# Turning x of the second half of the rows on VectorE and through a DRAM scratch instead of on TensorE

## The chip, the cores and the metric

The kernel runs on one core of a Trainium2 chip. The metric is the device time of one execution in microseconds (us). Before the change it is 1184.43 us, the median of 3 runs (1184.28 to 1184.72). The profile was taken from another execution of the same program, of 1184.46 us; the span from its first to its last instruction is 1182.7 us.

A core has five engines with an instruction queue each, and each queue is worked off in order: TensorE (PE in the profile, its weight loads PEld), VectorE (DVE), ScalarE (ACT), GpSimd (POOL) and SyncE (SP), which here does nothing but issue transfers (DMAs). Matmul results land in PSUM, which only VectorE and ScalarE empty in this kernel.

## The reference

One transformer layer with an attention branch and a feed-forward branch in parallel, 2048 rows of width 576, all in float32:

```python
xn  = layernorm(x)                       # over the 576 columns, no weights
qkv = xn @ wqkv                          # 576 x 1728; 32 heads of width 18
# every row attends to 8 keys: itself and the rows 2, 4, ..., 14 before it
logits = einsum(q, k at those rows) * 18 ** -0.5     # -1e9 before row 0
o   = softmax(logits) @ (v at those rows)
out = x + o @ wo + relu(xn @ w1) @ w2    # w1: 576 x 4608, w2: 4608 x 576
```

The attention looks back in steps of 2, so rows of even and of odd number never meet.

## The kernel before, in words

**Two parities.** The rows are worked in two halves (`ph` 0 and 1, the two parities of the row number), one after the other. A half has 8 tiles of 128 rows (`i`), taken in pairs as 4 token blocks of 256 rows (`tb`).

**Three products for one.** Every float32 operand is split into a high part (rounded to the type `fp32r`, on ScalarE) and a low part (what is left, by a subtraction on VectorE). A product is high x high + low x high + high x low. The width 576 is 4 blocks of 128 and 64 columns over; the last 64 are held twice in one block, as high and low (`mix`). One product over 576 is so 14 matmuls, in the order of the list `TERMS`: high parts of the moving side first, low parts after them, and so on.

**Slots.** The work is written out by hand as 288 slots, `slots[n]`: for each half, 12 chunks (`c`) of the 36 blocks of the 4608 hidden columns, for each chunk 4 token blocks, for each of these 3 hidden blocks (`f`). Half 1 begins with slot 144. In step n TensorE does the hidden product of slot n + 2 (`h_mm`, 14 matmuls into `ph`, PSUM, 2 buffers) and the output product of slot n (`o_mm`, 12 matmuls into `po`, PSUM). Between them ScalarE takes `hhi` (relu, L476) and VectorE `hlo` (L477) out of `ph`; the hidden product of slot m + 2 needs the buffer that these two release in slot m. After every third slot VectorE adds two `po` banks to x in place (L500), which releases them to the next slot's output product.

**What lies beside.** Into the slots are put, by the tables `at` (ahead of the output product) and `late` (after it): the q, k, v products; the attention itself, on VectorE (`run_bg`, as much as an estimate of VectorE's and TensorE's times allows); the product with `wo`; the loading and splitting of weights, staged three ahead in a pool of four buffers (`st`); and the making of the next half's x.

**The product with wo (slots 123 to 136 of half 0).** The attention's output for tile i has to be turned. `wo_a` turns it in 32 x 32 blocks on VectorE into the tile `tr` (L417, L418; one buffer), and four DMAs write `tr` to a DRAM scratch (`turned`) so that the blocks end up in their places (L424). `wo_f`, a slot later, reads the scratch back (L431). `wo_s`, at the end of the slot after that, splits what came into high (ScalarE, L438) and low (VectorE, L439, L440). `wo_b`, in the next slot, is the product: 28 matmuls into two `pm` banks, of which the first 8 read the high part and the next 8 the low part, and VectorE adds both to x (L453). `wo_a` of tiles 6 and 7 stands in slots 132 and 133, `wo_s` of them in 134 and 135, `wo_b` in 135 and 136. A new `wo_a` may write `tr` only when the four writes of the one before have landed.

**x of half 1 (slots 126 to 150).** For tile i, with z = 135 + 2i: the load in slot z - 6; the row statistics (`stats`) at the end of slot z - 2: four VectorE instructions (L245 twice, L246, L247), and on GpSimd the negated mean (L249) and the power -1/2 of the variance (L250); the normalising on VectorE (`norm`, L261) a slot later, so that GpSimd's part has a slot's time; and in slot z + 1 `make_xt`: five transposes on TensorE (L275, L276) into `pm`, a copy for the high part on ScalarE (L278, L280) and a subtraction on VectorE for the low (L279, L281). They go into `XT`, of which four are held, one for each token block; half 1 takes a block's buffer over as soon as half 0's last hidden product from it is done. Half 1's first hidden products, from token block 0, stand in step 142, those of block 1 in step 145, then 148 and 151.

Of the kernel before, what the change touches and what calls it, by code (L numbers as in the profile page):

```python
# [10 lines left out]
F32 = mybir.dt.float32  # L11
F32R = mybir.dt.float32r
AF = mybir.ActivationFunctionType
ALU = mybir.AluOpType
# [3 lines left out]
P = 128  # L18
# [3 lines left out]
TBN = 256  # L22
W = 8
# [4 lines left out]
EPS = 1e-5  # L28

UNIT0, UNIT_STEP, WO_AT = 7, 27, 8  # L30
WO_STEPS = (0, 1, 3, 4, 6, 7, 9, 10)
HEADW = (-5, -2, -1, 0, 0, 1)

# [23 lines left out]
def tile_body(ctx: ExitStack, tc: tile.TileContext, x, wqkv, wo, w1, w2, out):  # L57
    nc = tc.nc
    S, D = x.shape
    F = w1.shape[1]  # L60
    Dh = 18
    UD = HG * Dh
    NF = F // P
    NCH = NF // C
    KT = 4
    DR = D - KT * P
# [27 lines left out]
    f32 = lambda ap: ap.bitcast(F32)  # L94
# [22 lines left out]
    def dve(n):  # L117
        t["dve"] += (n + 130) / 960.0
# [112 lines left out]
    X, XT, XN, MR = {}, {}, {}, {}  # L231
# [34 lines left out]
    def transpose_split(src, last, hi, mix, lo, free=False):  # L266

        if free:
            pa, pb = (ps_o.tile([P, 2, 512], F32, name="po")[:, 0, :] for _ in range(2))
            pa, pb = pa.rearrange("p (k c) -> p k c", k=KT), pb[:, 0:P]  # L270
        else:
            pa = ps_m.tile([P, KT, P], F32, name="pm")
            pb = ps_m.tile([P, P], F32, name="pm")
        for k in range(KT):
            nc.tensor.transpose(pa[:, k, :], src[:, k * P : (k + 1) * P], ident)  # L275
        nc.tensor.transpose(pb, last, ident)  # L276
        t["pe"] += 5 * 0.06
        nc.scalar.activation(hi, pa, AF.Copy)  # L278
        nc.vector.tensor_tensor(lo, pa, f32(hi), op=ALU.subtract)  # L279
        nc.scalar.activation(mix, pb, AF.Copy)  # L280
        nc.vector.tensor_tensor(mix[DR:P], pb[DR:P], f32(mix[DR:P]), op=ALU.subtract)  # L281
        dve(512)
        dve(128)

    def make_xt(ph, i, free=False):
        tb, h = divmod(i, 2)
        if h == 0:
            XT[ph, tb] = xtp.tile([P, 9, TBN], F32R, name="xT")
        d = XT[ph, tb][:, :, h * P : (h + 1) * P]
        xn = XN.pop((ph, i))  # L290
        transpose_split(xn[:, 0:512], xn[:, 512:640], d[:, 0:4, :], d[:, 4, :], d[:, 5:9, :], free)


    TERMS = [(k, k) for k in range(KT)] + [(5 + k, k) for k in range(KT)] + [(4, 4)] + [(k, 5 + k) for k in range(5)]


    QO, KK, VV = {}, {}, {}

    def qkv_tile(ph, u, i):
# [106 lines left out]

    OT = {}

    TD = {}

    def wo_a(ph, i):


        assert (ph, i) in ready, (ph, i, len(bg))
        o = QO[ph][:, i, :]
        tr = tmp.tile([P, 640], F32, name="tr", bufs=1)
        nc.vector.transpose(tr[:, 0:D], o)  # L417
        nc.vector.transpose(tr[:, D:640], o[:, KT * P : D])  # L418
        dve(D)
        dve(DR)  # L420
        TD[ph, i] = turned.tile([5 * 4, 32, P], F32, name="turned")
        for r in range(4):
            rows = slice(32 * r, 32 * r + 32)
            nc.sync.dma_start(  # L424
                TD[ph, i][:, :, rows].rearrange("g j i -> j g i"),
                tr[rows, :].rearrange("j (g i) -> j g i", i=32),
            )

    def wo_f(ph, i):
        OT[ph, i] = tmp.tile([P, 5, P], F32R, name="xn", bufs=3)  # L430
        nc.sync.dma_start(f32(OT[ph, i]), TD.pop((ph, i)).rearrange("(k c) j i -> (c j) k i", k=5))  # L431

    def wo_s(ph, i):

        r = OT[ph, i]
        z = f32(r)
        d = tmp.tile([P, 5, P], F32R, name="oT", bufs=1)
        nc.scalar.activation(d, z, AF.Copy)  # L438
        nc.vector.tensor_tensor(r[:, 0:KT], z[:, 0:KT], f32(d[:, 0:KT]), op=ALU.subtract)  # L439
# [3 lines left out]
        OT[ph, i] = [d[:, k] for k in range(5)] + [r[:, k] for k in range(4)]  # L443
# [64 lines left out]
    def at(n, f, *a):  # L508
        todo.setdefault(n, []).append((f, a))
# [3 lines left out]
    def late(n, f, *a):  # L513
        todo_late.setdefault(n, []).append((f, a))

    plan = []
    for ph in range(NPH):
        b = ph * SPP
        for c in range(NCH):
            for f in range(C):  # L520
                s = b + c * SPC + f
                first = ph == c == 0
                plan.append((HEADW[f] if first else s - 5, w1_task, ((ph, c, f), c * C + f)))
                plan.append((HEADW[3 + f] if first else s - 3, w2_task, ((ph, c, f), c * C + f)))
        for u in range(NU):
            s = b + UNIT0 + u * UNIT_STEP
            plan.append((s - 5, wq_tasks, ((ph, u), u)))
            for i in range(NI):
                at(s + i, qkv_tile, ph, u, i)
            late(s + NI + 1, attention, ph, u)  # L530
        s = b + UNIT0 + NU * UNIT_STEP + WO_AT
        plan.append((s - 8, wo_tasks, (ph,)))
        for i in range(NI):
            z = s + WO_STEPS[i]
            late(z, wo_a, ph, i)
            at(z + 1, wo_f, ph, i)
            late(z + 2, wo_s, ph, i)
            at(z + 3, wo_b, ph, i)
            at(z + 3, done, ph, i)
        if ph + 1 < NPH:  # L540
            e = b + SPP - SPC
            for i in range(NI):
                z = e + 3 + 2 * i
                at(z - 6, load_x, ph + 1, i)
                late(z - 2, stats, ph + 1, i)
                late(z - 1, norm, ph + 1, i)
                at(z + 1, make_xt, ph + 1, i)
    for step, f, a in sorted(plan, key=lambda z: z[0]):
        if f in (wq_tasks, wo_tasks):
            f([step + k for k in range(5)], *a)  # L550
# [67 lines left out]
```

## Time and profile before

| what | value |
|---|---|
| median of 3 runs | 1184.43 us (1184.28 to 1184.72) |
| the profiled execution | 1184.46 us, span 1182.7 us |
| TensorE busy | 1174.6 us, 99% of the span, 8936 matmuls |
| VectorE busy | 822.3 us, 70%, 1301 instructions |
| ScalarE busy | 306.9 us, 26%, 758 instructions |
| GpSimd busy | 40.1 us, 3%, 63 instructions |
| the 56 + 14 transposes into `pm`, the 8 + 2 into `po` (both halves) | first at 6.5 us, the last at 623.9 us |
| writes to the scratch (L424) | 64, 80 KB each, 2.3 us from issue to landing (median) |
| reads from it (L431) | 16, 320 KB each, 3.2 us |

The profile's lines name an engine, a line of the kernel (L275), the operation, and what is written from what (`pm<-ident,xn`); behind them stand busy time and mean duration, or, in a timeline, the start and the length of a stretch of like instructions, in us from the span's start. In square brackets stands how long the engine was idle just before and who ended that. "PEclk" is the clock that TensorE was granted, as a share of the full one. Busy times of TensorE are modelled from pipelined matmuls, so lengths of neighbouring stretches overlap a little, and it is the distance of their starts that counts.

### The profile page before, as it was taken

What the parts mean: (1) busy time and instruction counts of PE and PEld (TensorE: products, weight loads), DVE (VectorE), ACT (ScalarE), POOL (GpSimd) and SP (SyncE); (2) the same over time, 40 slices, a digit from 0 to 9 for tenths busy, and PEclk for the clock granted to TensorE, in tenths of its full rate; (3) what the DMA queues carried; (4) which work ended last, traced back from release to release, by engine and by line L of the source; (5) the groups of instructions that cost most, each with busy time, mean ns of one, the idle gap of its engine ahead of it and who ended that gap; (6) DMA issues with size and microseconds to landing.
All of it is one profiled execution on the core that took longest, in us unless ns stands there. A gap on an engine that the chain in (4) does not pass through costs nothing.

```text
span 1182.7 us, 21731 instructions
## 1 busy us (share of the span) xinstructions
PE 1174.6 (99%) x8936; PEld 1164.9 (98%) x8936; DVE 822.3 (70%) x1301; ACT 306.9 (26%) x758; POOL 40.1 (3%) x63
## 2 busy tenths in 40 slices
PE   8999999999999999999999999999999999999998
PEld 8999999999999999999999999999999999999998
DVE  7516885888687668877673288758777884787852
ACT  5422222131222211322233123121322222222210
POOL 2000000010000000000020000000100000000000
PEclk9999999999999999999999999999999999999999
DMA  5312121130312211356342122121302213114541
GB/s 174 85 32 79 39 84 47 47 108 1 99 45 58 65 55 44 104 112 148 105 131 74 47 55 80 32 77 27 98 21 80 70 43 89 47 30 110 115 100 60
DMA packets 137364, 86.16 MB, mean 73 GB/s; under 512 B 48832, under 2 KB 120768, under 8 KB 137264
## 3 DMA queue, kind: packets, MB, share of 16 engines
q1 hardware_dynamic: 134736, 76.58, 24.0%
q10 hardware_dynamic: 2528, 8.20, 2.4%
q8 instruction: 70, 1.15, 0.4%
q14 instruction: 30, 0.25, 0.1%
HBM read 66.58 MB, written 9.96 MB: 65 GB/s over the span
## 4 chain that ended last, share of the span: by engine, by line
PE 95%; DVE 2%; DMA 2%; ACT 0%; SPq 0%; issue 0%; POOL 0%; DVEq 0%; ACTq 0%
PE ph L114 37%; PE po L114 37%; PE pm L114 20%; DMA st<-in_w 1%; DMA xn<-turned 1%; PE pm L275 0%; DVE pr L382 0%; DMA turned<-tr 0%; DVE x L500 0%; DMA x<-in_x 0%; DVE pr L345 0%; SPq L424 0%; DVE w1t L145 0%; DVE w2t L145 0%; DVE bst L245 0%
## 5 line engine op out<-in xcount | busy, mean ns | idle before, releaser
L114 PE MATMUL ph<-xT,w1t 128*128 128x256 f32 x4032 | 513.0, 278 | 1.3 <-ACT xT L278 0.6
L114 PEld LDWEIGHTS ph<-xT,w1t 128*128 128x128 f32 x4032 | 491.9, 188 | 2.1 <-ACT xT L278 0.8
L114 PE MATMUL po<-w2t,hhi 128*128 128x288 f32 x2304 | 400.7, 296 | 0.6 <-DVE w2t L145 0.3
L114 PEld LDWEIGHTS po<-w2t,hhi 128*128 128x128 f32 x2304 | 336.9, 188 | 2.4 <-issue 0.5
L476 ACT ACTIVATE hhi<-ph 128x256 fp32r<-128x256 f32 x288 | 110.1, 382 | 553.5 <-PE ph L114 538.2
L114 PE MATMUL po<-w2t,hlo 128*128 128x288 f32 x1152 | 244.7, 293 | 0.0
L477 DVE SCALAR_TENSOR_TENSOR hlo<-ph,hhi 128x256 fp32r<-128x256 f32 x288 | 121.5, 422 | 161.0 <-ACT hhi L476 160.1
L500 DVE TENSOR_TENSOR x<-po,x 128x576 f32<-128x576 f32 x192 | 143.4, 756 | 69.9 <-PE po L114 67.0
L114 PE MATMUL pm<-wq,xT 128*128 128x432 f32 x896 | 185.5, 358 | 0.0
L114 PEld LDWEIGHTS po<-w2t,hlo 128*128 128x128 f32 x1152 | 183.6, 188 | 0.0
L114 PEld LDWEIGHTS pm<-wq,xT 128*128 128x128 f32 x896 | 163.8, 188 | 5.6
L145 DVE TENSOR_TENSOR w2t<-st,w2t 128x576 fp32r<-128x576 f32 x72 | 54.3, 755 | 45.6 <-ACT w2t L148 45.4
L345 DVE TENSOR_TENSOR pr<-qo,k 128x1152 f32<-128x1152 f32 x64 | 85.8, 1349 | 0.0
L348 DVE TENSOR_REDUCE lg<-pr 128x64 f32<-128x1152 f32 x64 | 84.9, 1343 | 0.0
L375 DVE TENSOR_TENSOR pr<-lg,v 128x1152 f32<-128x1152 f32 x64 | 84.7, 1350 | 0.2
L382 DVE TENSOR_TENSOR pr<-pr 128x288 f32<-128x288 f32 (+1 forms) x128 | 70.6, 601 | 0.1
L145 DVE TENSOR_TENSOR w1t<-st,w1t 128x640 fp32r<-128x640 f32 x72 | 59.0, 820 | 13.8 <-ACT w1t L148 13.7
L148 ACT ACTIVATE w2t<-st 128x576 fp32r<-128x576 f32 x72 | 49.1, 683 | 57.2 <-PE po L114 42.4
L314 ACT ACTIVATE k<-pm 128x144 f32<-128x144 f32 x64 | 18.6, 291 | 143.9 <-PE pm L114 143.9
L148 ACT ACTIVATE w1t<-st 128x640 fp32r<-128x640 f32 x72 | 53.0, 736 | 11.4 <-DMA st<-in_w 11.4
L351 POOL TENSOR_SCALAR_AFFINE_SELECT lg<-lg 1x512 f32<-1x512 f32 x8 | 9.4, 1171 | 844.1 <-DVE lg L348 844.1
L114 PE MATMUL pm<-wq,oT 128*128 128x288 f32 x224 | 35.2, 296 | 0.3 <-ACT oT L438 0.3
(61 smaller groups left out, 444.7 us busy)
## 6 DMA issues: line engine op xcount, KB each, us to landing
st<-in_w SPq DMA_DIRECT2D x72, 288.0 KB, 3.0
st<-in_w SPq DMA_DIRECT2D x72, 256.0 KB, 3.0
st<-in_wqkv SPq DMA_DIRECT2D x32, 216.0 KB, 3.0
turned<-tr SPq DMA_DIRECT2D x64, 80.0 KB, 2.3
xn<-turned SPq DMA_DIRECT2D x16, 320.0 KB, 3.2
st<-in_w SPq DMA_DIRECT2D x144, 32.0 KB, 2.7
out<-x SPq DMA_DIRECT2D x16, 288.0 KB, 2.1
x<-in_x SPq DMA_DIRECT2D x15, 288.0 KB, 3.6
```

Of the source, the lines that this page charges most:

```text
L114: nc.tensor.matmul(o, l, r, start=start, stop=stop)
L145: nc.vector.tensor_tensor(lo, src, f32(hi), op=ALU.subtract)
L148: nc.scalar.activation(hi, src, AF.Copy)
L314: nc.scalar.activation(k[:, W - 1 + i, :], pq[:, 1, :], AF.Copy)
L345: nc.vector.tensor_tensor(pr[i], q, window(k, i), op=ALU.mult)
L348: nc.vector.tensor_reduce(lg[:, i], pr.pop(i).rearrange(heads, d=Dh), axis=AX.X, op=ALU.add)
L351: nc.gpsimd.affine_select(out=z, in_=z, pattern=[[1, NI], [1, W], [0, HG]], compare_op=ALU.is_ge, fill=-1e9 / scale, base=1 - W, channel_m ...
L375: nc.vector.tensor_tensor(pr[i].rearrange(heads, d=Dh), e, window(v, i).rearrange(heads, d=Dh), op=ALU.mult)
L382: nc.vector.tensor_tensor(o, z[:, 0:n], z[:, n : 2 * n], op=ALU.add)
L476: nc.scalar.activation(hi, pt, AF.Relu)
L477: nc.vector.scalar_tensor_tensor(lo, pt, 0.0, f32(hi), op0=ALU.max, op1=ALU.subtract)
L500: nc.vector.tensor_tensor(acc, PO[k][:, :, 0:D2], acc, op=ALU.add)
```

## The change

For half 1 the five TensorE transposes of every tile are replaced by the way that `wo` already goes: `turn` (two VectorE transposes into `tr`, four DMAs to the scratch) and `fetch` (one DMA back, straight into `XT`). `xt_s` then splits what lies in `XT` in place. The table `XT_STEPS` says, for every tile, how far from slot 132 (`e`) the load, the statistics with the normalising, the turning (`send`), the reading back (`back`) and the splitting (`parts`) stand. Statistics and normalising, a slot apart before, stand one behind the other in the same slot. The normalised x lies in a buffer of the attention's products (`pr`) instead of `xn`. The pool of x tiles has 12 buffers instead of 11, the scratch 4 instead of 3. In `XT` and in `wo`'s split tile high and low parts change places, and `TERMS` with them, so that every product still has the same 14 matmuls on the same parts in the same order. Half 0's x is still turned on TensorE.

```diff
+XT_STEPS = (
+    (-6, 0, 0, 2, 6),
+    (-5, 1, 2, 4, 8),
+    (-3, 2, 3, 5, 9),
+    (-1, 4, 5, 7, 11),
+    (4, 6, 7, 9, 13),
+    (5, 8, 9, 11, 14),
+    (7, 10, 11, 13, 16),
+    (8, 11, 12, 14, 17),
+)
...
-    xp = pool("xp", 11)
+    xp = pool("xp", 12)
...
-    turned = pool("turned", 3, space=bass.MemoryType.DRAM)
+    turned = pool("turned", 4, space=bass.MemoryType.DRAM)
...
+    def turn(o, td):
+        tr = tmp.tile([P, 640], F32, name="tr", bufs=1)
+        nc.vector.transpose(tr[:, 0:D], o)
+        nc.vector.transpose(tr[:, D:640], o[:, KT * P : D])
+        dve(D)
+        dve(DR)
+        for r in range(4):
+            rows = slice(32 * r, 32 * r + 32)
+            nc.sync.dma_start(
+                td[:, :, rows].rearrange("g j i -> j g i"),
+                tr[rows, :].rearrange("j (g i) -> j g i", i=32),
+            )
+
+    def fetch(z, td):
+        nc.sync.dma_start(z, td.rearrange("(k c) j i -> (c j) k i", k=5))
+
+    def norm_turned(ph, i):
+        nm, r = MR.pop((ph, i))
+        XN[ph, i] = prp.tile([P, W, UD], F32, name="pr").rearrange("p w c -> p (w c)")[:, 0:D]
+        nc.vector.tensor_scalar(XN[ph, i], X[ph, i], nm, r, op0=ALU.add, op1=ALU.mult)
+        dve(600)
+
+    def xt_a(ph, i):
+        TD[ph, i] = turned.tile([5 * 4, 32, P], F32, name="turned")
+        turn(XN.pop((ph, i)), TD[ph, i])
+
+    def xt_f(ph, i):
+        tb, h = divmod(i, 2)
+        if h == 0:
+            XT[ph, tb] = xtp.tile([P, 9, TBN], F32R, name="xT")
+        fetch(f32(XT[ph, tb][:, 0:5, h * P : (h + 1) * P]), TD.pop((ph, i)))
+
+    def xt_s(ph, i):
+        tb, h = divmod(i, 2)
+        d = XT[ph, tb][:, :, h * P : (h + 1) * P]
+        z = tmp.tile([P, 5, P], F32R, name="oT", bufs=1)[:, 0]
+        mix = d[:, 4, :]
+        nc.scalar.activation(d[:, 5:9, :], f32(d[:, 0:4, :]), AF.Copy)
+        nc.vector.tensor_tensor(d[:, 0:4, :], f32(d[:, 0:4, :]), f32(d[:, 5:9, :]), op=ALU.subtract)
+        nc.scalar.activation(z[DR:P], f32(mix[DR:P]), AF.Copy)
+        nc.vector.tensor_tensor(mix[DR:P], f32(mix[DR:P]), f32(z[DR:P]), op=ALU.subtract)
+        nc.scalar.activation(mix[0:DR], f32(mix[0:DR]), AF.Copy)
+        dve(512)
+        dve(128)
...
             e = b + SPP - SPC
             for i in range(NI):
-                z = e + 3 + 2 * i
-                at(z - 6, load_x, ph + 1, i)
-                late(z - 2, stats, ph + 1, i)
-                late(z - 1, norm, ph + 1, i)
-                at(z + 1, make_xt, ph + 1, i)
+                load, first, send, back, parts = (e + k for k in XT_STEPS[i])
+                at(load, load_x, ph + 1, i)
+                late(first, stats, ph + 1, i)
+                late(first, norm_turned, ph + 1, i)
+                late(send, xt_a, ph + 1, i)
+                at(back, xt_f, ph + 1, i)
+                at(parts, xt_s, ph + 1, i)
```

More of the change, by code (lines that the diff above doesn't have):

```diff
@@ L290, in make_xt @@
         xn = XN.pop((ph, i))
[L291 to L294 removed]
+        transpose_split(xn[:, 0:512], xn[:, 512:640], d[:, 5:9, :], d[:, 4, :], d[:, 0:4, :], free)
+    TERMS = (
+        [(5 + k, k) for k in range(KT)] + [(k, k) for k in range(KT)] + [(4, 4)]
+        + [(5 + k, 5 + k) for k in range(KT)] + [(4, 9)]
+    )
[10 more added lines that the diff above has]
+                tr[rows, :].rearrange("j (g i) -> j g i", i=32),
+            )
+    def fetch(z, td):
[25 more added lines that the diff above has]
+        dve(128)
+    TD = {}
     QO, KK, VV = {}, {}, {}
@@ L407, in tile_body @@
     OT = {}
-    TD = {}
     def wo_a(ph, i):
         assert (ph, i) in ready, (ph, i, len(bg))
[L415 to L420, printed above, removed]
-        TD[ph, i] = turned.tile([5 * 4, 32, P], F32, name="turned")
[L422 to L427, printed above, removed]
+        TD[ph, i] = turned.tile([5 * 4, 32, P], F32, name="turned")
+        turn(QO[ph][:, i, :], TD[ph, i])
     def wo_f(ph, i):
         OT[ph, i] = tmp.tile([P, 5, P], F32R, name="xn", bufs=3)
-        nc.sync.dma_start(f32(OT[ph, i]), TD.pop((ph, i)).rearrange("(k c) j i -> (c j) k i", k=5))
+        fetch(f32(OT[ph, i]), TD.pop((ph, i)))
     def wo_s(ph, i):
@@ L442, in wo_s @@
         dve(128)
-        OT[ph, i] = [d[:, k] for k in range(5)] + [r[:, k] for k in range(4)]
+        OT[ph, i] = [r[:, k] for k in range(KT)] + [d[:, KT]] + [d[:, k] for k in range(KT)]
     def wo_b(ph, i):
```

## The prediction

> **What bounds the kernel now.** I read the busy times first, then who kept TensorE waiting, then the timeline of the stretch that the change touches (slots 131 to 151, about 541 to 627 us).
>
> ```profile
> PE 1174.6 (99%) x8936; PEld 1164.9 (98%) x8936; DVE 822.3 (70%) x1301; ACT 306.9 (26%) x758; POOL 40.1 (3%) x63
> ...
> PE pm L275 <- DVE x L453: 0.4, 1, 0.4
> ```
>
> TensorE is the bound: the waits that its list names come to 2.4 us once it has begun, and 0.4 us of that lies in the stretch in question (second line). So a matmul taken away is time won, and any wait that TensorE gets in its place is time lost. TensorE's timeline, start and length in us:
>
> ```profile
> 580.13 1.78 PE L114 MATMUL ph<-xT,w1t 128*128 128x256 f32 x14
> 581.75 0.60 PE L275 MATMUL pm<-ident,xn 128*128 128x128 f32 x4
> 582.19 0.27 PE L276 MATMUL pm<-ident,xn 128*128 128x128 f32 x1
> 582.22 0.78 PE L114 MATMUL po<-w2t,hhi 128*128 128x288 f32 x4
> ...
> 583.89 1.78 PE L114 MATMUL ph<-xT,w1t 128*128 128x256 f32 x14
> ...
> 587.09 1.78 PE L114 MATMUL ph<-xT,w1t 128*128 128x256 f32 x14
> ```
>
> From one hidden product to the next a slot with transposes takes 3.75 us (583.89 - 580.13), one without 3.20 (587.09 - 583.89). Then VectorE and TensorE around the last products with wo, and VectorE's load in six slots further on (busy, instructions, clock, DMA):
>
> ```profile
> 504.58 0.20 DVE L418 STREAM_TRANSPOSE tr<-qo 128x64 f32<-128x64 f32 x1
> ...
> 508.51 0.78 DVE L417 STREAM_TRANSPOSE tr<-qo 128x576 f32<-128x576 f32 x1 [1.68 <-DMA turned<-tr]
> ...
> 553.01 0.20 DVE L418 STREAM_TRANSPOSE tr<-qo 128x64 f32<-128x64 f32 x1
> ...
> 562.80 0.68 DVE L439 TENSOR_TENSOR xn<-xn,oT 128x512 fp32r<-128x512 f32 x1
> ```
>
> ```profile
> 563.54 1.22 PE L114 MATMUL pm<-wq,oT 128*128 128x288 f32 x8
> 564.60 1.23 PE L114 MATMUL pm<-wq,xn 128*128 128x288 f32 x8
> ```
>
> ```profile
> 583.89:603.00 19.11, 15.25 (x32) 1.00 0.48 151
> ```
>
> The first two lines show a turning held up, since `tr` has one buffer: from the end of L418 (504.78) until the writes have landed and L417 may start again, 3.73 us. The third is wo tile 6's turning, done at 553.21. The low part of tile 6 is ready at 563.48 (L439) and wanted at 564.60: only 1.1 us to spare. And in the six slots from 583.89 VectorE is already busy for 15.25 of 19.11 us.
>
> **What goes.** The transposes of eight tiles: seven slots shrink by 0.55 us, and the first (slot 136, 568.85 to 576.95, 8.10 us, against 6.91 for the one ahead of it, 561.93 to 568.85) by 1.19, the 0.4 us wait included: 7 x 0.55 + 1.19 = **5.0 us won**, all on TensorE.
>
> **What is added at no price.** ScalarE's three instructions for a tile (0.60, 0.27, 0.26 us) become three of such sizes, and it is 26% busy. SP issues five more DMAs for each tile (4 x 0.51 + 0.38 = 2.4 us, 20 us in some 50); behind them stand weight loads, staged three ahead and landing in 3.0 us, and outputs. I take 0; without that cover, one landing too late costs at most 1 us, and nothing of it can win time. The read back stands 3 to 5 slots (9.6 us and more) ahead of the split and lands in 3.2 us; the splits stand two slots and more ahead of the first use; `XT`'s buffers are free two slots before. The `pr` buffers are free: the last attention instruction ahead of slot 132's work ends at 547.99.
>
> **First wait: tile 6 of wo, slots 132 to 135.** VectorE's order in slot 132 becomes: wo tile 6's turning, x tile 0's statistics and normalising, x tile 0's turning; in slot 133 wo tile 7's turning, x tile 1's statistics and normalising; and only at the end of slot 134 tile 6's L439. Three turnings now follow on one `tr`. The trip from the end of a turning to the free `tr` is 3.73 us (504.78 to 508.51; by the read that waits for the same writes, 553.21 to 556.94 and 1142.46 to 1146.20) to 4.26 (558.86 to 563.12); mean of five, 3.93. From 553.21: trip 3.93; turning 0.90 (552.31 to 553.21); trip 3.93 (hlo and two L453 hide in it), so wo tile 7 turns at 561.97. Then 0.90; statistics 1.21 (558.78 to 559.99); a wait for GpSimd of 0.7, because the normalising now follows at once (L250's 0.57 and two hand-overs); normalising 0.55; hlo 0.37; two L500 1.34; L439 0.68: 567.7. Wanted at 564.60, so TensorE waits **3.1 us** (2.7 by the short trips, 3.8 by the long). The read of tile 6, now behind eight writes on SP's queue, lands at about 563.2 and its high part is ready near 564.0, 0.5 after TensorE wants it; that wait lies inside the 3.1.
>
> **Second wait: the bank release in slot 143.** From hlo in slot 138 on VectorE has work without a break. Up to slot 143's first L500, which releases the bank that slot 144's output product writes: 6 hlo at 0.35, 4 splits at 1.05 (576.08 to 577.13), 3 statistics with GpSimd's wait and the normalising at 2.50, 3 w1 subtractions at 0.75, 3 of w2 at 0.68, 2 turnings at 0.82, two L500 1.34 and one 0.75: 2.1 + 4.2 + 7.5 + 2.25 + 2.04 + 1.64 + 2.09 = 21.8 us. The hlo starts 2.2 us after its slot (576.95 to 579.16), and slot 144's output product 6 x 3.20 + 1.61 = 20.8 us after it, so there are 18.6 us: TensorE waits **3.2 us** (2.5 to 3.6, for 0.1 us more or less in each of the splits and hand-overs). Before, the six slots held three tiles' work, without the waits for GpSimd. The backlog goes on: slot 146's L500 would come about 0.5 us late (one more trip, 3.9, after the turning in slot 143).
>
> **What the clock makes of the waits.** Here the trace has a row at its beginning: TensorE's gaps, then windows (us; busy PE, PEld, DVE, ACT, POOL; granted clock):
>
> ```profile
> 9.11 0.74 PE L114 MATMUL ph<-xT,w1t 128*128 128x256 f32 x4 [0.58 <-ACT xT L278]
> 10.42 1.98 PE L114 MATMUL ph<-xT,w1t 128*128 128x256 f32 x7 [0.57 <-DVE xT L279]
> ```
>
> ```profile
> 10.00:10.50 0.50, 0.08 (x1) 0.08 (x1) 0.47 (x2) 0.50 (x1) 0.00 (x0) 1.00 0.98 217
> 10.50:11.00 0.50, 0.50 (x3) 0.50 (x4) 0.47 (x2) 0.41 (x2) 0.00 (x0) 0.66 1.07 326
> 11.00:11.50 0.50, 0.50 (x4) 0.38 (x2) 0.50 (x2) 0.47 (x2) 0.00 (x0) 0.50 0.93 304
> ...
> 13.50:14.00 0.50, 0.50 (x4) 0.50 (x3) 0.50 (x2) 0.07 (x1) 0.00 (x0) 0.50 1.00 332
> 14.00:14.50 0.50, 0.50 (x6) 0.50 (x6) 0.50 (x2) 0.50 (x2) 0.00 (x0) 0.93 0.94 369
> ```
>
> After gaps of 0.17, 0.58 and 0.57 us (1.3 us within 3.4) the clock was halved from about 10.66 to 14.07, 3.4 us, though TensorE worked all through it. A wait of 3.1 us puts at least half of itself, 1.55, into one stretch of 3.4 us wherever that begins, more than the 1.3. So I charge each wait one halved stretch: 3.4 / 2 = **1.7 us**, twice (nothing if the clock holds; 2.6 if a stretch begins inside the wait and the next is halved too: (3.4 - 1.55 + 3.4) / 2). The slower TensorE gives VectorE 1.7 us, which takes up the 0.5 of slot 146.
>
> [...]
>
> **Sum.** -5.0 + 3.1 + 1.7 + 3.2 + 1.7 = +4.7 us. The profiled execution is 1184.46 us, 0.03 from the median, so the sum stands for the median too: **1189.1 us**. Its own range, 1186.7 (short trips, 2.5, 1.0 us for each halving) to 1190.6.
>
> **Rivals.**
> - *The clock holds.* [...] For it: at 574.75 a gap of 0.42 us left the clock at 1.00. Against it: the rows above. -5.0 + 3.1 + 3.2 + 0.5 = +1.8: 1186.2 us (1184.9 to 1187.3), for the most part not slower by 0.2%.
> - *The clock stays low longer.* 2.6 for each wait: -5.0 + 3.1 + 2.6 + 3.2 + 2.6 = +6.5: 1190.9 us. Each wait is near a stretch's length, so the start of one often falls inside; against it, the clock came back after one stretch of work.
> - *VectorE is not late, and the 5.0 us are kept:* 1179.4 us. VectorE's 21.8 us would have to be under 18.6, and wo tile 6 on time as well, two trips shorter by 3.1 us together; the fastest landing of these DMAs, 1.8 us against 2.4, gives 1.2. With only one of the waits gone, and its halving, the sum is about -0.1: no change.
>
> **Chances.** My forecast 0.51, clock holds 0.24, clock low longer 0.15, kept gain 0.06, others 0.04. Faster by over 0.2% (2.4 us, about what this kernel's measurement tells from no change): 0.06. Within 0.2%: 0.17 of the second case and 0.04 of others and of my own low end, 0.21. Slower: 0.73. The range 1184.6 to 1191.6 leaves out the kept gain and the tails of the rest.
>
> **What the new profile would show.** No transposes after the first 60 us, slots without them 3.20 us apart. TensorE waiting about 3 us for the low part of a wo tile near 565 us, and about 3 us for an L500 near 605, by the old lines' names. L417 waiting for DMA in slots 132 and 133. VectorE idle before the normalising for 0.7 us, eight times. The granted clock at 0.50 for some 3.4 us after each long wait. It is wrong if TensorE waits less than 2.7 us in that stretch, if the clock stays at 1.00 after a wait of 3 us, or if a wait stands where I charged nothing: at `XT`, at a weight load or at SP.

## The result, and the profile after

The changed kernel took 1192.22 us (median of 6 runs, 1191.59 to 1195.27), the kernel before, on the same chip, 1184.81 us (6 runs, 1184.28 to 1185.95): a ratio of 1.0065, with a 95% interval from 1.0054 to 1.0076. It is slower by 7.4 us, where 4.7 had been forecast. The profiled execution of after took 1192.14 us, span 1190.3 us, 7.7 more than before's (1190.34 - 1182.67).

The page's line of busy times, and the longest waits of TensorE (engine and line, releaser, us in total, times, longest):

```profile
PE 1171.5 (98%) x8896; PEld 1161.6 (98%) x8896; DVE 827.3 (69%) x1317; ACT 308.4 (26%) x758; POOL 38.9 (3%) x63
```

```profile
PE po L125 <- DVE x L549: 4.8, 2, 3.1
PE pm L125 <- ACT oT L487: 3.9, 3, 2.1
PE pm L125 <- DVE xn L488: 1.4, 1, 1.4
```

The 40 matmuls are gone, and TensorE now waits for two engines. L549 is the old L500 (x += po), L487 and L488 the old L438 and L439 (the split of a wo tile), L314 the old L417 (the turning), L526 the old L477. Where these waits stand, in TensorE's timeline of after:

```profile
564.75 1.33 PE L125 MATMUL pm<-wq,oT 128*128 128x288 f32 x8 [1.41 <-ACT oT L487]
...
567.52 2.29 PE L125 MATMUL pm<-wq,xn 128*128 128x288 f32 x8 [1.45 <-DVE xn L488]
...
608.66 0.78 PE L125 MATMUL po<-w2t,hhi 128*128 128x288 f32 x4 [3.05 <-DVE x L549]
...
620.29 0.76 PE L125 MATMUL po<-w2t,hhi 128*128 128x288 f32 x4 [1.77 <-DVE x L549]
...
1103.66 1.33 PE L125 MATMUL pm<-wq,oT 128*128 128x288 f32 x8 [2.12 <-ACT oT L487]
```

The first two are wo tile 6, the third is the bank of slot 143, the fourth that of slot 146, and the fifth is the first wo tile of half 1, in a stretch that the change does not touch (before: 0.26 us). VectorE in the same stretches:

```profile
557.32 0.78 DVE L314 STREAM_TRANSPOSE tr<-pr 128x576 f32<-128x576 f32 x1 [2.08 <-DMA turned<-tr]
...
561.91 0.78 DVE L314 STREAM_TRANSPOSE tr<-qo 128x576 f32<-128x576 f32 x1 [2.64 <-DMA turned<-tr]
...
566.79 0.68 DVE L488 TENSOR_TENSOR xn<-xn,oT 128x512 fp32r<-128x512 f32 x1
...
611.88 1.16 DVE L331 TENSOR_SCALAR pr<-x,nm,rstd 128x576 f32<-128x576 f32 x1 [0.76 <-POOL rstd L261]
...
615.33 0.78 DVE L314 STREAM_TRANSPOSE tr<-pr 128x576 f32<-128x576 f32 x1 [1.96 <-DMA turned<-tr]
...
1099.61 0.78 DVE L314 STREAM_TRANSPOSE tr<-qo 128x576 f32<-128x576 f32 x1 [3.60 <-DMA turned<-tr]
```

Wo tile 7 turns at 561.91 (forecast 561.97), and the low part of tile 6 comes at 566.79 + 0.68 = 567.47 (567.7). The trip that ends at 615.33 began at 609.99 and took 5.3 us, the one that ends at 1099.61 began at 1093.96 and took 5.65 us; in the kernel before the same trip of half 1 took 3.73. The clock, in windows of 3.41 us (busy PE, PEld, DVE, ACT, POOL; granted clock; DMA share; GB/s):

```profile
563.15:566.56 3.41, 1.51 (x10) 1.09 (x8) 2.65 (x8) 1.01 (x2) 0.75 (x2) 1.00 0.58 105
566.56:569.97 3.41, 2.45 (x10) 2.45 (x11) 3.17 (x9) 0.00 (x0) 0.21 (x2) 0.50 0.67 199
569.97:573.38 3.41, 3.41 (x16) 3.41 (x15) 1.73 (x4) 0.60 (x1) 0.54 (x2) 0.50 1.05 262
604.11:607.52 3.41, 1.50 (x14) 1.30 (x12) 2.58 (x7) 0.57 (x2) 0.75 (x2) 1.00 0.74 171
607.52:610.93 3.41, 2.27 (x18) 2.30 (x19) 3.34 (x8) 0.00 (x0) 0.00 (x0) 1.00 0.84 276
```

After the waits of wo tile 6 the clock is halved for two such windows (second and third row), and after the wait of 3.05 us not at all (fourth and fifth). The account of this execution:

| part | forecast, us | measured, us | from |
|---|---|---|---|
| transposes gone | -5.0 | -5.0 | kernels of the last two experiments, see below |
| waits of wo tile 6 | +3.1 | +2.9 | 1.41 + 1.45 |
| half clock after them | +1.7 | +2.9 | (6.82 halved - 0.96 of it waiting) / 2 |
| bank of slot 143 | +3.2 | +3.05 | L549 at 608.66 |
| half clock after it | +1.7 | 0 | 1.00 throughout |
| bank of slot 146 | 0 | +1.8 | L549 at 620.29 |
| half 1's first wo tile | 0 | +1.9 | 2.12 - 0.26 |
| slots 129 to 153, not accounted for | 0 | +0.6 | 6.2 us longer in all, less the rows above |
| rest of the span | 0 | -0.4 | ahead of slot 129 it ran 0.37 us ahead |
| sum | +4.7 | +7.7 | of 7.7 in the span |

The first row does not come out of this profile alone. From ScalarE's `hhi` of one slot ahead of the change's stretch (519.61 us before, 519.24 after) to one behind it (627.48 and 633.32) the changed kernel takes 6.2 us more, and the waits and the half clock in it come to 10.6: that leaves 4.4 us won, not 5.0. Where the missing 0.6 went is not shown. In the kernels below that keep at most one wait in this stretch, the same sum, with any half clock and added products counted, leaves 4.9 to 5.0.

### The profile page after: what moved, and what is told of

Read it like the earlier page. It is cut to its first block, busy times and chain, and to the rows that moved or that the text cites. A ratio compares the mean times of both kernels' runs of the same rounds, so it can differ in the third digit from the quotient of the medians.

```text
span 1190.3 us, 21730 instructions
## 1 busy us (share of the span) xinstructions
PE 1171.5 (98%) x8896; PEld 1161.6 (98%) x8896; DVE 827.3 (69%) x1317; ACT 308.4 (26%) x758; POOL 38.9 (3%) x63
## 4 chain that ended last, share of the span: by engine, by line
PE 92%; DVE 3%; DMA 2%; SPq 1%; issue 1%; ACT 1%; POOL 0%; DVEq 0%; ACTq 0%; POOLq 0%
PE po L125 36%; PE ph L125 36%; PE pm L125 20%; DMA turned<-tr 1%; SPq L320 1%; DMA st<-in_w 1%; DMA xn<-turned 1%; DVE tr L314 0%; DVE x L549 0%; DMA x<-in_x 0%; DVE hlo L526 0%; DVE bst L256 0%; DVE xT L351 0%; ACT oT L487 0%; DVE pr L446 0%
## 5 line engine op out<-in xcount | busy, mean ns | idle before, releaser
L526 DVE SCALAR_TENSOR_TENSOR hlo<-ph,hhi 128x256 fp32r<-128x256 f32 x288 | 121.0, 420 | 156.4 <-ACT hhi L525 155.7
L549 DVE TENSOR_TENSOR x<-po,x 128x576 f32<-128x576 f32 x192 | 143.2, 756 | 70.1 <-PE po L125 67.2
L439 DVE TENSOR_TENSOR pr<-lg,v 128x1152 f32<-128x1152 f32 x64 | 84.6, 1347 | 0.2
```

The source lines that it names most:

```text
L439: nc.vector.tensor_tensor(pr[i].rearrange(heads, d=Dh), e, window(v, i).rearrange(heads, d=Dh), op=ALU.mult)
L526: nc.vector.scalar_tensor_tensor(lo, pt, 0.0, f32(hi), op0=ALU.max, op1=ALU.subtract)
L549: nc.vector.tensor_tensor(acc, PO[k][:, :, 0:D2], acc, op=ALU.add)
```

## The experiments

My theory when they began: VectorE is late twice, once because three turnings queue on one `tr`, once because its work does not fit; the half clock follows from the waits. The rivals: the clock is halved whatever TensorE does, or the waits come from the trips of the scratch rather than from VectorE's load. The last line of TensorE's timeline was unexplained, and became a theory of its own.

**The same kernel again.**

> The changed kernel once more, for a second profile of it. Theory (VectorE is late at two places, TensorE waits there, and some waits are followed by a halved clock): 1191 to 1195 us; again a wait of 2.5 to 3.5 us in all for wo tile 6, one of about 3 us for the L549 of slot 143 and one of 1 to 2 us for that of slot 146; halved clock for 1 to 5 stretches of 3.4 us, not the same ones as in the first profile, since the two waits of 3 us had 6.8 and 0 us of it there. Rival (the first profile shows an accident, above all its 2.1 us wait in the wo product of half 1): that wait stays in this one too, or the three others are gone. By the theory the 2.1 us wait is an accident of one long trip and is below 1 us here.

Measured: 1194.22 us (1193.16 to 1195.17, 4 runs), 1.0077 (1.0062 to 1.0092). Waits came back at all five places, one of them small (1.74 and 1.49 at wo tile 6, 3.06 for slot 143, 0.20 for slot 146, 2.14 in half 1). So the wait in half 1 is no accident of one execution, as I had thought it could be. The clock differs: three halvings in the kernel's middle here, among them one after the wait of 3.06 us, and the wait of slot 146 shrank there to 0.20 us. In the two runs below that also have a half clock just behind the wait for slot 143 (28 and 8 transposes ahead of half 1) no wait over 0.2 us stands at slot 146, which fits: the slower TensorE gives VectorE the time.

```profile
565.32:568.73 3.41, 1.33 (x8) 1.09 (x8) 2.75 (x5) 0.96 (x2) 0.63 (x2) 1.00 0.47 82
568.73:572.14 3.41, 3.26 (x13) 3.27 (x14) 2.59 (x9) 0.00 (x0) 0.75 (x2) 0.50 0.91 279
606.28:609.69 3.41, 0.84 (x6) 0.88 (x7) 3.35 (x7) 0.00 (x0) 0.00 (x0) 1.00 0.77 232
609.69:613.10 3.41, 3.41 (x18) 3.41 (x17) 2.58 (x7) 0.00 (x0) 1.82 (x4) 0.50 0.90 237
```

In this execution the halved windows begin at 568.73, 609.69 and 1104.62 us, and one in the kernel's first 20 us at 12.36: 163.0, 12.0 and 145.0 windows of 3.413 us apart. One window is as long as the halved stretch at the start of the kernel before (10.66 to 14.07), and within this execution all four lie on one raster. How long TensorE idled in a window of it, and the clock in the next:

| execution | window from | TensorE idle, us | clock in the next |
|---|---|---|---|
| after | 563.15 | 1.90 (1.41 + 0.49) | 0.50 |
| after | 604.11 | 1.91 of the 3.05 | 1.00 |
| after | 607.52 | 1.14, the rest of it | 1.00 |
| after | 617.76 | 1.77 | 1.00 |
| again | 565.32 | 2.08 | 0.50 |
| again | 606.28 | 2.57 of the 3.06 | 0.50 |
| again | 1101.20 | 2.14 | 0.50 |

In the kernel's middle, over these and the experiments below whose raster can be read: nine windows with 2.06 to 2.73 us idle were each followed by a halved one (the three above, 2.72 and 2.73 with own buffers, 2.59 with 28 transposes ahead of half 1, 2.06 and 2.07 with 8, 2.24 with own buffers and early statistics), ten with 1.14 to 1.77 by none (two above, 1.21 from 1102.45 in after, 1.31 and 1.71 with 28 transposes ahead of wo tile 6, 1.57 and 1.63 with 28 ahead of half 1, 1.71 with 8, 1.66 with early statistics, 1.48 with own buffers and early statistics), and of the two with 1.90 and 1.91 one was. A window at half clock was followed by another one in the three cases with 0.73 (8 transposes), 0.96 (after) and 1.00 us (8 transposes) idle in it, by the full clock in those with up to 0.46. So the wait of 3.05 us, cut by the raster into 1.91 and 1.14, was followed by the full clock, and the one of 3.06, with 2.57 in one window, by the half clock. Between executions the raster lies differently: the first halved window begins 10.66 us into the span in the kernel before and 12.36 here, 1.70 us or half a window apart.

**Buffers of their own for x's turnings.**

```diff
-        turn(XN.pop((ph, i)), TD[ph, i])             # into tr, 1 buffer
+        turn(XN.pop((ph, i)), TD[ph, i], "xn", 3)    # into xn, 3 buffers
```

The rotation `xn` of three buffers also takes wo's read backs.

> x's turnings write to a buffer of another rotation (three buffers) instead of wo's single tr, nothing else. Theory (the wait for wo tile 6 comes from three turnings queueing on one tr, 2.1 + 2.6 us of VectorE's waiting for the scratch writes): that wait of 2.9 us goes to under 0.5, its halved clock (3.15 us) goes with it, the 2 us wait ahead of the turning in slot 144 goes too and with it 1 us or more of the 1.8 us wait of slot 146; the wait of slot 143 stays at about 3 us. 1192.2 - 2.9 - 3.1 - 1.2 = 1185.0 us, 1183.5 to 1187. Rival (VectorE has simply too much work there, whoever waits for tr): the wait for wo tile 6 stays at 2 us or more and the time above 1190.

Measured: 1187.58 us (1185.72 to 1188.72, 10 runs), 1.0021 (1.0012 to 1.0030), a little above the range expected and 6.6 us below the repeat of the changed kernel, which ran beside it.

```profile
563.70 1.22 PE L125 MATMUL pm<-wq,oT 128*128 128x288 f32 x8
564.75 1.23 PE L125 MATMUL pm<-wq,xn 128*128 128x288 f32 x8
...
603.18 0.76 PE L125 MATMUL po<-w2t,hhi 128*128 128x288 f32 x4 [3.06 <-DVE x L549]
```

Wo tile 6 comes without a wait, and slot 146's wait is gone too; the one for slot 143 stays at 3.06. So the first wait is the single `tr`, and the second is not. What I had not counted on: half 1's wo wait, 2.7 us here, and a half clock after both (idle 2.72 and 2.73 us in one window).

**The statistics a slot ahead.**

```diff
-                late(first, stats, ph + 1, i)
+                late(first - (i > 2), stats, ph + 1, i)
```

> The statistics of x tiles 3 to 7 stand one slot ahead of their normalising again, so that GpSimd's part has a slot's time; nothing else. Theory (VectorE's idle 0.7 us ahead of each normalising is part of the crowd of slots 138 to 143): three of these waits, 2.1 us, leave the crowd, and the wait of slot 143 falls from 3.1 to 1.0 to 1.9 us; the wait for wo tile 6 with its halved clock stays, slot 146's stays or grows by little. 1190.0 to 1191.5 us. Rival (the crowd's length is set by something else, as ScalarE's copies or late weights, and VectorE only idles in another place): the wait of slot 143 stays at 3 us, 1192 us.

Measured: 1192.42 us (1190.83 to 1193.86, 4 runs), 1.0062 (1.0045 to 1.0078): no gain. The wait for slot 143 fell from 3.05 to 0.30 us, but a new one of 2.40 us stands at 596.25, one group of three slots earlier, and it gives VectorE 2.4 us more for all that follows. So this run does not show what the statistics are worth. TensorE, and then VectorE:

```profile
596.25 1.26 PE L125 MATMUL po<-w2t,hhi 128*128 128x288 f32 x4 [2.40 <-ACT xT L354]
```

```profile
591.28 0.78 DVE L314 STREAM_TRANSPOSE tr<-pr 128x576 f32<-128x576 f32 x1 [2.95 <-DMA turned<-tr]
...
595.35 1.42 DVE L549 TENSOR_TENSOR x<-po,x 128x576 f32<-128x576 f32 x2
```

The turning before it ended at 584.25, so this trip took 7.0 us, VectorE stood still in front of the single `tr`, and everything behind was late, L549 among it. The profile names ScalarE's split of an x tile (L354) as what ended the wait; the first of the two L549 ended less than 0.2 us ahead of it, and which of the two chains would have held TensorE alone is not shown.

**TensorE kept busy ahead of wo tile 6.** 28 transposes of the identity, written into the bank that the product then overwrites:

```diff
+        if (ph, i) == (0, 6):
+            for _ in range(28):
+                nc.tensor.transpose(po[0][:, 0:P], ident, ident)
```

> 28 transposes of the identity, 3.1 us of TensorE's time at full clock, stand ahead of wo tile 6's product in slot 135, into the bank that the product overwrites; all else is the changed kernel. They do work that nobody needs, while TensorE would wait. Theory (it is the idling that is followed by the half clock): the 2.9 us of waiting become work, no halved stretch follows, and the time falls though TensorE does more: 1192.2 - 3.1 + 0.3 = 1189.4 us, 1188.3 to 1190.5. Rival (the half clock there has nothing to do with the wait): the halved 6.8 us stay and the time is 1192 to 1193 us.

Measured: 1187.77 us (1186.18 to 1189.66, 10 runs), 1.0027 (1.0018 to 1.0037), below the range expected. Work added in front of the product made the kernel 6.5 us faster than the repeat beside it. The wait is gone, and so is every halving in the profiled execution's middle, which agrees with idling as the cause but is weak evidence by itself: in two of the five profiled executions that have the wait of wo tile 6 no halving followed it either (the largest idle time in a window was 1.66 us in one and 1.63 in the other), and the wait for slot 143, 3.02 us here, was cut by the raster into 1.71 and 1.31. But a part was a surprise: half 1's wait had fallen from 2.1 to 0.24 us, though nothing is different there but 56 TensorE instructions that had gone by.

**What lengthens the trip in half 1.** The DMA view holds a second queue, "q8 instruction". Within the trip of half 1's first wo tile, before (1088.19 to 1091.92):

```profile
q1 hardware_dynamic: 2624, 0.33, 50.4%
```

and after (1093.96 to 1099.61; packets, MB, share of 16 engines):

```profile
q1 hardware_dynamic: 2624, 0.33, 33.6%
q8 instruction: 1, 0.02, 1.6%
```

One packet of 0.02 MB, by its queue's name a stretch of program, was fetched during the write. The page of after has 70 of them, one for 2 x 8896 / 70 = 254 of TensorE's matmuls and weight loads, about one in 17 us. If they do it, added instructions must move them. So the same transposes, 28 or 8, were put far ahead, at half 1's first q, k, v product:

```diff
+        if (ph, u, i) == (1, 0, 0):
+            for _ in range(FILL):        # 28 or 8
+                nc.tensor.transpose(pq.rearrange("p a b -> p (a b)")[:, 0:P], ident, ident)
```

> 28 transposes of the identity (56 TensorE instructions) are added ahead of the first q/k/v product of half 1, into a bank that the product then overwrites; nothing else moves. Theory: the trip of the first wo tile of half 1 through the scratch took 5.6 us instead of 3.7 because one instruction fetch (0.02 MB, the row 'q8 instruction' of the DMA view) fell into its write, at 3.4 us after the start of the turning (2.6 us in the write); such fetches come once in some 15 us, about every 256 TensorE instructions, and in the kernel before it fell 1.3 us ahead of the turning. 56 instructions move it 3.1 to 3.3 us earlier, to about 0.3 us after the start of the turning, ahead of the write: trip 3.7 to 4.0 us, the wait for ScalarE's oT near slot 267 0.2 to 0.5 us instead of 2.1, and no halved clock behind it. The added work costs 28 x 0.056 = 1.6 us, so about 1191.5 us, from 1190 to 1193. Rival (the trip is longer because of the scratch's fourth buffer, or because of what the change left on SP's queue): trip 5.6 us and wait 2.1 us as before, and 1.6 us more: about 1194.5.

> The same with 8 transposes (16 instructions): the fetch moves only some 0.9 us earlier, to about 2.5 us after the start of the turning, and still falls into the write. Theory: trip 5.2 to 5.7 us, wait near slot 267 1.7 to 2.2 us; the added work costs 0.45 us: about 1193.3 us, from 1192 to 1195. Rival (any disturbance of TensorE's order there shortens the trip, not the place of the fetch): trip 3.7 to 4.0 us as in the run with 28.

Measured: 1192.62 us with 28 (4 runs, 1.0070, 1.0056 to 1.0084), 1192.97 us with 8 (4 runs, 1189.35 to 1195.36, 1.0071, 1.0051 to 1.0091). A transpose cost 0.106 us, so 28 took 3.0 us; the 0.056 that these two expectations add up with, and those with 88 transposes and with the table below, stands in no trace or run. The times tell nothing apart; the trips do. With 28:

```profile
1099.24 0.78 DVE L315 STREAM_TRANSPOSE tr<-qo 128x576 f32<-128x576 f32 x1 [2.00 <-DMA turned<-tr]
```

and with 8:

```profile
1102.47 0.78 DVE L315 STREAM_TRANSPOSE tr<-qo 128x576 f32<-128x576 f32 x1 [3.36 <-DMA turned<-tr]
```

With 28 the trip took 4.05 us (from 1095.19) and TensorE's wait 0.53; with 8 it took 5.41 (from 1097.06) and the wait 1.72, as the theory said of both to within 0.05 us. That left open whether the kernel before would suffer the same.

**The fetch moved in the kernel before**, with 88 and with 102 transposes at the same place:

> The kernel before with 88 transposes of the identity (176 TensorE instructions) ahead of the first q/k/v product of half 1, overwritten by that product. They move the fetches 10.4 us earlier against the work, that is, the one that fell 1.3 us ahead of the turning of half 1's first wo tile gives place to the next, at about 3.4 us after its start. Theory: the kernel before gets what the change brought by accident: trip 5.4 to 5.8 us instead of 3.73, wait for ScalarE's oT near slot 267 2.0 to 2.6 us instead of 0.3; with 88 x 0.056 = 4.9 us of added work about 1191.2 us in all (up to 1193 with a halved clock behind the wait). Rival (the longer trip belongs to the changed kernel's scratch or queue): trip 3.7 to 4.0 us, wait 0.3 us, about 1189.2.

> As the run with 88 transposes in the kernel before, with 102: there the next fetch came 4.5 us after the start of the turning, just behind the write, and the trip stayed at 3.74 us; 14 transposes more move it 1.5 us earlier, to about 3.0 us, into the write. Theory: the kernel before, with nothing of the change in it, gets the long trip, 5.0 to 5.7 us, and a wait of 1.5 to 2.4 us for ScalarE's oT near slot 267; a transpose cost 0.106 us there, so 102 take 10.8 us, and the time is about 1197 us (up to 1199 with a halved clock). Rival (the long trip belongs to the changed kernel, with its fourth scratch buffer and its other queue): trip 3.7 to 4.0 us, no wait above 0.4 us, about 1195.

With 88 (1193.35 us, one run) the forecast of a long trip missed: the fetch began 3.6 us after the end of the turning, when the write was all but done, and the trip stayed at 3.74. As the fetch had not fallen where it was aimed, the run does not decide. With 102 (1196.59 us, one run) the fetch fell into it:

```profile
1108.10 1.32 PE L115 MATMUL pm<-wq,oT 128*128 128x288 f32 x8 [1.81 <-ACT oT L442]
```

Trip 5.47 us, wait 1.81, in a kernel with nothing of the change in it. So this part of the loss is an accident of where a fetch falls, and not of the fourth scratch buffer or of what the change left on SP's queue. All trips of half 1's first wo tile, by the start of the fetch against the end of the turning:

| run | fetch, us | trip, us |
|---|---|---|
| before | -1.9 | 3.73 |
| table with 28 small products (below) | -0.8 | 3.71 |
| table with 28 transposes (below) | -0.8 | 3.72 |
| own buffers, early statistics, 28 transposes (below) | -0.6 | 3.72 |
| 28 ahead of wo tile 6 | -0.6 | 3.81 |
| after, 28 added | -0.1 | 4.05 |
| before, 102 added | +1.3 | 5.47 |
| after, 8 added | +2.4 | 5.41 |
| after | +3.0 | 5.65 |
| own buffers, early statistics (below) | +3.0 | 5.92 |
| after, the same kernel again | +3.1 | 5.83 |
| own buffers | +3.2 | 5.82 |
| early statistics | +3.3 | 5.81 |
| table (below) | +3.3 | 5.70 |
| before, 88 added | +3.6 | 3.74 |

The trip of 5.3 us in front of slot 146 is another case: a fetch began at 611.5, 1.5 us into it. The run with the transposes ahead of wo tile 6 is the counter-test: there the same turning, at the same distance behind the wait for slot 143, meets no fetch. Its trip took 4.18 us, 1.2 less, and the wait of slot 146 was 0.62 instead of 1.77, 1.2 less too, with the clock at 1.00 in both.

In half 0 a trip can be long without a fetch as well: the one behind the turning that ended at 570.08 in the second profile of the changed kernel took 5.51 us, and no fetch began in it, but the queue moved 1.34 MB in that time, of which the four writes are 0.33. In the trip of 7.0 us above SP took 4.51 us to issue its four writes instead of 2.04, and the issuing was slow before the first fetch in it began (at 587.2).

**Both causes in half 0 removed, and another table.** First the own buffers and the early statistics together, then the own buffers with a new table, in which the statistics have a column of their own:

```diff
-    (-6, 0, 0, 2, 6), (-5, 1, 2, 4, 8), (-3, 2, 3, 5, 9), (-1, 4, 5, 7, 11),
-    (4, 6, 7, 9, 13), (5, 8, 9, 11, 14), (7, 10, 11, 13, 16), (8, 11, 12, 14, 17),
+    (-6, 0, 0, 1, 3, 7), (-5, 0, 2, 3, 5, 9), (-1, 2, 2, 4, 7, 10), (2, 3, 3, 4, 7, 11),
+    (4, 5, 6, 7, 10, 13), (4, 5, 6, 10, 12, 15), (7, 9, 11, 11, 13, 16), (8, 11, 12, 13, 15, 18),
```

> x's turnings in buffers of their own (three, shared with wo's read backs) and the statistics of tiles 3 to 7 one slot ahead of the normalising. Theory (the two waits in half 0 are VectorE's, one from the single buffer, the other from 21.8 us of VectorE's work with 0.7 us idle ahead of each normalising): neither wait near wo tile 6 nor the one of 3.05 us for the bank of slot 143 (at most 1 us), so 3 us below the run with buffers of their own alone: about 1184.5, from 1182 to 1187, the upper part if a late read back stops TensorE as it did with the early statistics alone (2.4 us), or if the fetch falls into half 1's first wo write (2.7 us). Rival (taking the idle time from ahead of the normalising only moves VectorE's work earlier into a stretch that is full): a wait of 2 us or more at another place in slots 132 to 150, and about 1187.5.

> Buffers of their own for the turnings, a slot of its own for the statistics, and another table of slots: statistics 0, 0, 2, 3, 5, 5, 9, 11, normalising 0, 2, 2, 3, 6, 6, 11, 12, turning 1, 3, 4, 4, 7, 10, 11, 13, read back 3, 5, 7, 7, 10, 12, 13, 15, parts 7, 9, 10, 11, 13, 15, 16, 18. Theory: the time of the change is that of its waits on VectorE, and the 5.0 us of the transposes are a gain once none is left: no wait of TensorE over 1 us in slots 132 to 154, and 1180 to 1183 us where the fetch misses half 1's first wo write, up to 2.7 us more where it falls into it. Rival (the added work of VectorE, ScalarE and the queue does not fit beside the slots, whatever the table): waits of 2 us or more in slots 132 to 154 and 1184.5 us or more.

Measured: 1184.60 us for both (10 runs, 1182.84 to 1186.54; 1.0003, 0.9994 to 1.0012), 1184.13 us for the table (11 runs, 1181.86 to 1186.06; 0.9996, 0.9987 to 1.0005). TensorE's longest waits with the table:

```profile
PE pm L125 <- ACT oT L487: 2.5, 1, 2.5
...
PE po L125 <- DVE x L549: 1.3, 1, 1.3
```

And with both, where the own buffers alone had 3.06:

```profile
601.32 0.78 PE L125 MATMUL po<-w2t,hhi 128*128 128x288 f32 x4 [1.80 <-DVE x L549]
```

In half 0 only 1.3 us (1.8 for both) are left, above the 1 us expected; the rest is the fetch in half 1's trip. With no other wait in half 0, the step from 3.06 to 1.80 shows what the early statistics are worth: 1.3 us, not the 2.1 that I had expected of them.

**The fetch moved away from the trip.** 28 transposes of the identity in the kernel with the table, and in the one with both, ahead of the hidden product that stands before the wait for slot 143; then, with the table, 28 products of 32 x 32 in their place:

```diff
+        if n == SPP + LAG:
+            for _ in range(28):
+                nc.tensor.transpose(pt[:, 0:P], ident, ident)
+                # or: nc.tensor.matmul(pt[0:32, 0:32], xt[:, 0, 0:32], xt[:, 0, 0:32], start=True, stop=True)
```

> The spread table with 28 transposes of the identity ahead of the hidden product that stands before slot 144's output product, where TensorE still waited 1.31 us for the bank of slot 143; they are written into the bank that this hidden product then overwrites. Theory: they take 1.57 us, of which 1.3 us lie in that wait, and move every later instruction fetch 3.3 us earlier, so that the fetch that fell 4.0 us after the start of half 1's first wo turning (trip 5.7 us, wait 2.5 us) comes at about 0.7 us, ahead of the write: trip 3.8 to 4.1 us, wait at most 0.6 us, no halved clock behind either: 1182.4 us, from 1181 to 1183.5, and faster than before. Rival (the wait in half 1 has another cause in this table, or the fetch now meets another trip that something waits for): 1184.4 us or more.

> The same 28 transposes in the kernel that has the turnings' own buffers and the early statistics (wait for the bank of slot 143 1.80 us, fetch 3.8 us after the start of half 1's first wo turning, wait 2.6 us). Theory: the transposes lie in the wait of 1.8 us, the fetch comes at about 0.5 us, trip 3.8 to 4.1 us, wait at most 0.6 us: about 1182.3 us, from 1181 to 1183.8. Rival as for the spread table: 1184.5 us or more.

> The spread table with 28 products of 32 x 32 in place of the 28 transposes, at the same place: as many TensorE instructions (56), and less time. The transposes took 3.0 us, of which the wait for the bank of slot 143 hid 1.3; the small products should take 0.8 to 1.5 us and lie in that wait whole. Theory (the fetches go by the number of TensorE's instructions, not by its time): the fetch stays ahead of half 1's first wo write as in the run with the transposes (trip 3.8 to 4.1 us, wait at most 0.6 us), and the time is 1.5 to 1.7 us less: about 1180.4 us, from 1179.5 to 1182. Rival (small products cost as much as the transposes, by the load of their weights): about 1182, as that run.

Measured: 1181.94 us with the table (11 runs, 1181.49 to 1183.26; 0.9982, 0.9973 to 0.9991), 1183.05 us with both (11 runs; 0.9985, 0.9975 to 0.9994), and with the small products 1180.88 us (7 runs, 1180.22 to 1182.23), beside 1184.56 us of the kernel before: 0.9968, from 0.9957 to 0.9979. This last one is faster than both kernels of this document. The transposes, and the small products:

```profile
597.67 3.22 PE L523 MATMUL ph<-ident 128*128 128x128 f32 x28
```

```profile
597.91 1.04 PE L523 MATMUL ph<-xT 128*32 128x32 f32 x28
...
601.17 0.76 PE L126 MATMUL po<-w2t,hhi 128*128 128x288 f32 x4 [0.53 <-ACT hhi L529]
```

From the start of the 28 to the next product 2.97 us passed with the transposes (600.64 - 597.67) and 0.89 with the small ones (598.80 - 597.91). The trip was 3.72 and 3.71 us, with 2.1 us between the two fillings, and the fetch began 0.8 us ahead of the turning's end in both: here the number of instructions placed the fetch, not their time. At the place of the wait for slot 143, 0.53 us are left beside the small products, now for ScalarE's `hhi`, and of the 5.0 us won 3.7 are kept.

## Why the prediction was right and wrong

- **The transposes, -5.0:** right, by the kernels that keep at most one wait in the stretch (4.9 to 5.0). In the changed kernel itself 0.6 us of it is missing, and the cause stays open.
- **The first wait, +3.1:** right in mechanism and size (2.86). Own buffers removed it. Its parts were less well placed: TensorE waited 1.41 us for the high part, charged with 0.5, and 1.45 for the low part behind it.
- **The second wait, +3.2:** right (3.05), and its working too: from the `hlo` at 586.80 to the end of the first L549 at 608.51 VectorE took 21.7 us of the 21.8 charged, idle for three waits of 0.76 us for GpSimd and for hardly anything else. Those waits are part of it, but early statistics win back only 1.3 us of them (3.06 to 1.80).
- **"What the clock makes of the waits", +1.7 twice:** mis-sized. The halving is real, but a wait is not worth one stretch: it measured 2.9 after the first wait and 0 after the second, and in the next execution a halving after each. The step went wrong in reading the row at the kernel's start, a window idle for 39% that was followed by the half clock, as if it gave the limit for all windows. In the kernel's middle windows with 1.14 to 1.77 us idle (up to 52%) kept the clock, and a wait of 3.05 us fell once into one window with 2.57 us of it and once with 1.91. Nor did it hold at the kernel's start: in the run with 28 transposes ahead of half 1 the window from 5.96 us, idle for 1.42 us, kept the clock. What I charged as certain was a chance, and that 2.9 in all came near the 3.4 charged is luck.
- **"Slot 146 ... taken up", 0:** this step failed, +1.8. The step took one more trip at 3.9 us and a slower TensorE. The trip was 5.3, with a fetch in it, and the clock was not halved. Where it was (the same kernel again), the wait was 0.20 with a trip just as long, so the relief is as I had put it. Without the fetch (28 transposes ahead of wo tile 6) the wait was 0.62, near the 0.5 that the step had before its relief.
- **"What is added at no price", 0:** right for `XT`, `pr`, ScalarE and SP, where no wait came up. The step that failed is the trip of 3.73 to 4.26 us, and with it the silence on half 1's wo tile, where TensorE waited 0.26 us already: that was charged nothing, and cost 1.9. In the cases that I named for the range no fetch began after the turning. The profile of the kernel before held longer ones, by the same reading: from the end of the turning at 519.40 to its read back at 524.53 us are 5.1 us, with a fetch 1.4 us into the write, and from 536.20 to 541.20 are 5.0, with a fetch 0.2 us after the turning.
- **Two slips without weight:** the read backs stand 3 to 4 slots ahead of the splits, not 3 to 5, and the terms of the sum give 1190.3 for the upper end, not 1190.6.

So the direction and the two waits held, and the time came out 3.1 us above the forecast and just above its range, because the trip through the scratch was priced as if nothing else used the DMA engines: 1.8 + 1.9 us, less the 0.5 by which the clock cost less. The rival of the holding clock was half true in the profiled execution, and its price of 1186.2 was still far off, for the same reason. The kept gain was not this kernel's, but it is to be had.

## What to carry to other kernels

A round trip through a DRAM scratch needed slack here for a program fetch, about 2 us on 3.7, and for the other transfers on its queue. Without it 102 transposes added in the kernel before brought a wait of 1.81 us in a stretch that nobody had touched, and 28 added in the changed kernel took one of 2.12 down to 0.53; so an experiment's time has to be read place by place. Give a producer that is put in front of another its own buffer before moving slots: here a single-buffered tile cost a wait of 2.9 us, and with it the other remedy gained nothing. And price a stall on TensorE as the stall, plus the half clock as a chance: here it followed in nine windows of nine with 2.06 us or more idle of 3.413, and in none of ten with 1.14 to 1.77.

## What the runs showed of the hardware

- Where a fetch of program (one packet of the queue "q8 instruction", 0.02 MB) began 1.3 to 3.3 us after the turning, while four times 80 KB were written to the scratch, the way to the free buffer of half 1's first wo tile took 5.4 to 5.9 us (eight profiled executions); where one began ahead of the turning's end, or 3.6 us after it, 3.7 to 4.05 (seven).
- TensorE's granted clock was halved for 3.41 us from 10.66 us in the kernel before and for 6.83 us from 566.56 in the profile of after; in the second profile of the changed kernel the halved windows began 163.0, 12.0 and 145.0 times 3.413 us apart. In the kernel's middle nine such windows with 2.06 to 2.73 us idle were each followed by a halved one, ten with 1.14 to 1.77 by none, and one of the two with 1.90 and 1.91; a halved window was followed by the full clock with up to 0.46 us idle in it, and by another halved one with 0.73, 0.96 and 1.00.
- 28 transposes of 128 x 128 on TensorE took 106 ns each, 28 products of 128 x 32 by 32 columns 32 ns each, start to start.
- VectorE's normalising took 1.16 us instead of 0.58 while GpSimd cleared rows (from 611.79 to 613.92 us in the profile of after, and in the eight other profiled executions in which the two met).
